# Two tail loads in 256-byte pieces, and all engine orders planned anew

## The chip, the cores and the metric

One NeuronCore of a Trainium2 chip runs the whole program. The metric is device time in microseconds (us), the median of the runs shown; before the change it is 316.97 us. TensorE (PE) does the matmuls and transposes, VectorE (DVE), ScalarE (ACT) and GpSimd (POOL) do the element-wise work, and SyncE (SP) issues the loads and stores, which sixteen DMA engines carry out.

## The reference

Sliding-window attention feeds a two-layer block. There are 8 batches, 8 heads, 576 tokens and 64 numbers per head; inputs and output are float32.

```python
scores = q @ k.T / sqrt(64)                # per batch and head, 576 x 576
scores = where(abs(i - j) <= 32, scores, -1e9)
attn = softmax(scores)                     # over the last axis
x = (attn @ v)                             # heads side by side: 4608 x 512
h = maximum(x @ w_in, 0)                   # w_in 512 x 2048
out = (s * h * h + b) @ w_out              # w_out 2048 x 512, s and b are scalars
```

## The kernel before

All matmuls work on bf16 with float32 sums in PSUM, which the program divides into four tiles of two banks each: `w`, `o`, `sc` and `avn`. The program is not written in the order in which it runs. Each step is recorded as a task with `add` (stream, functions, an assumed cost, what it reads and writes, a key, and for loads a number of packets and a cost of each), and `_Graph.plan` then walks through time: it always takes the open task that could start first, with the key as tie-break, and so fixes one order for each of five streams (PE, ACT, DVE, POOL, SP). Some constants at the head of the file are such keys; others say which engine does a cast or a copy and which bank is used. `fill` looks for gaps that are planned on PE and puts dummy matmuls into them (`ONESW` times `ONESW`, of 128 columns at L563 or 512 at L564). `emit` turns dependencies into semaphore waits. At run time each engine keeps its order, and only the waits decide when something starts. A second path of the program runs only on inputs that the first one's sums flag as out of range.

The first 70 us differ from the rest, because nothing is loaded yet. Loads of batches 0 and 1 and of both weights go through SP in one firm order (keys under -100; the lists `ORDER0` and `ORDER1`). For each batch these are:

- four pairs of heads, for q and for k (`load_pair`, L724): 512 tokens, 256 KB, in packets of 1 KB, each into one of eight staging slots (`STG`);
- the last 64 tokens of all heads, q and k (`load_rest`, L737), called the tails here;
- v (L668, for batch 0 also L685).

Between them stand w_in and w_out (`load_weights`, L640) in chunks of 512 KB, two loads each, in packets of 2 KB. A firm load's number is its place in that order, counted from nought in the constants of the change; by the words "third" and "twelfth" the loads with numbers 2 and 11 are meant. Number 11 is the second load of w_in.

What is staged is cast to bf16 (L757 for q, k and tails, L643 for weights, L677 for v) and, for q and k, transposed on PE: `turn_pair` (L770, four 128 x 128 transposes, copied out at L776) and `turn_rest` (L788, copied out at L798 and L799). Scores follow (L1016, for the last tokens L1047), exponentials (L1061), the mask (L1066; for batch 0 the scores' banks are opened with the mask's large negatives instead, L1035), the product of weights and values (L940), the divisors (L964) and the normalising (L966), a transpose to `xt` (L973) and its copy (L981).

The slots are used in turn. The casts of batch 1's pairs are recorded after all firm loads, so where a slot is loaded twice, a pair's cast waits for the slot's second load: pair 2 for loads of w_out, pair 1 for the loads of pair 3, which are the last two pair loads of all.

The block's first product is `s1` (L1213), with relu on ACT (L1220) and the square on DVE (L1222); its second product is `s2` (L1231), put out with s and b at L1247 and stored. For the first 512 tokens the second product is cut into 32 groups of two matmuls, which add up in four banks (`o` and `avn`) and which PE takes up while it waits for loads (`early`, L1264); their results go out at L1276 (ACT) or L1279 (DVE). `colsum` (L1294) sums w_out's columns for the term with b.

From batch 2 on, q and k are transposed by DMA (`piece`); the first `XPE` units of attention have their results transposed on PE, the later ones by DMA.

The loads of the tails before, and the turn of the tails before, are these lines:

```python
stg[:, 256 * x:256 * x + 256],
src[b, :, BODY:S, :].rearrange("h (p i) d -> h p (i d)", i=ROWS)
...
tile[p0:p0 + 64, 64 * j:64 * j + 64].rearrange("p (a s) -> p a s", a=NPAIR), lhsT=nat[:, 64 * j:64 * j + 64],
```

Each load has 8 heads x 16 partitions, four tokens (1 KB) on a partition: 128 packets. The turn makes sixteen matmuls with pieces of the identity, each into 64 partitions.

Of the kernel before, what the change touches and what calls it, by code (L numbers as in the profile page):

```python
# [7 lines left out]
BF16 = mybir.dt.bfloat16  # L8
# [3 lines left out]
S = 576  # L12
D = 64
H = 8
DM = H * D
DFF = 2048
WIN = 32
NPAIR = H // 2
# [4 lines left out]
VW = 66  # L23
QB = 176
LAG = 1
SPLIT = (4, 3)
WHOLE = 9
SPREAD = ('act', 'dve', 'act', 'act')
K0 = ('dve', 'dve', 'pool', 'pool')
Q0 = ('dve', 'dve', 'act', 'dve')  # L30
# [3 lines left out]
PLACEK = (-28.3, -27.4, -24.3)  # L34
PLACEB = ('AVN', 'W', 'W')
BANK0 = ('AVN', 'SC', 'O', 'SC', 'O')
SCORE0 = ('SC', 'O', 'SC', 'O', 'SC')
OPENK = -55
LASTK = -21.3
WINE = ('dve', 'act', 'pool', 'pool')  # L40
TURNKEY = -18.5
TURN = (None, 0)
FIRST = ((0, 0), (None, 0), (1, 1), (0, 1), (1, 0), (0, 2), (1, 2), (2, 0), (2, 1), (2, 2), (0, 3), (2, 3), (None, 0), (None, 0), (None, 0), (1, 3), (None, 0))
WOUTE = (('act', 'pool'), ('act', 'pool'), ('act', 'dve'), ('pool', 'dve'))
TAIL = ('dve', 'act')
HOST = (("k", 3), ("q", 0))
HELD = (3400.0, 1200, 2800, 4000)
OPEN = -19.25
REST = ('dve', 'dve')
ORDER1 = (('w', 0), ('w', 1), ('p', 2), ('p', 1), ('p', 0), ('w', 3), ('w', 2), ('e', 0), ('p', 3), ('v', 2), ('v', 4), ('v', 3), ('v', 0), ('v', 1))  # L50
XTS = 2500
EARLYW = (('W', 0), ('W', 1), ('W', 0), ('AVN', 1), ('W', 1), ('AVN', 1), ('SC', 0), ('O', 0), ('O', 0), ('W', 1), ('AVN', 1), ('W', 1), ('AVN', 1), ('W', 1), ('SC', 0), ('W', 1), ('O', 1), ('W', 1), ('AVN', 0), ('AVN', 0))
SUMS = -20
PREP = -17.5
SUME = 'act'
SUMC = 'dve'
EARLYP = ('act', 'dve', 'dve', 'act')
ADDE = ('pool', 'dve', 'dve', 'dve')
ADDK = 11.0
SUMAT = 3  # L60
ROWS = 4
BODY = 128 * ROWS
XPE = 20
LEAD = 10.0
SIZES = (224, 128, 160, 256, 256)
PACE = ((-1, -1, -1),) * 3
CASTS = 40.0
LATE = 8
CASTE = (("pool", "pool"), ("pool", "pool"))
SLACK = (2500.0, 1000.0, 4500, 1000)  # L70
PACEV = ((-1,-1,0,0,1),(0,0,1,1,2),(0,0,1,1,2))
EV0 = ('act', 'pool', 'act', 'act', 'act')
BANK1 = ('SC', 'W', 'O', 'SC', 'AVN')
EV1 = ('pool', 'dve', 'pool', 'pool', 'dve')
EV2 = ('pool', 'pool', 'pool', 'dve', 'dve')

ACT_TABLE_SET_ID = 6
FAR = 1e38
COPYQ = (('act', 'dve', 'act', 'dve'), ('act', 'act', 'dve', 'act'))
COPYK = (('dve', 'act', 'act', 'act'), ('dve', 'act', 'act', 'act'))  # L80
XTE = ('dve', 'act', 'act', 'dve', 'act', 'act', 'act', 'act', 'dve', 'dve', 'act', 'act', 'dve', 'act', 'act', 'act', 'act', 'act', 'dve', 'act')
TURN1 = (1, 0, 3, 1, 2, 3, 0, 2, 1)
SCORE1 = ('SC', 'SC', 'SC', 'W')
FIRSTQK = (('qk', 'kq', 'kq', 'qk'), ('qk', 'qk', 'qk', 'kq'))
K1 = ('pool', 'dve', 'dve', 'dve')
Q1 = ('pool', 'pool', 'pool', 'dve')
SUMBANK = ("W", 1)
WARM = 5
LEAST = 2.0 ** -60
AHEAD = {"pe": 48, "act": 180, "dve": 240, "pool": 240}  # L90

# [17 lines left out]
class _Graph:  # L109
# [55 lines left out]
    def plan(self):  # L165
# [5 lines left out]
        for t in self.tasks:  # L171
            for d in t.deps:
                d.users.append(t)
        open_ = {s: [t for t in self.tasks if t.left == 0 and t.stream == s] for s in self.STREAMS}
        order = []
        shape, pair = "full", {"dve": 0.0, "pool": 0.0}
# [53 lines left out]
        while len(order) < len(self.tasks):  # L230
            best = None
            for s in self.STREAMS:
                for t in open_[s]:
# [14 lines left out]
            t = best[1]  # L248
# [29 lines left out]
        while any(rings.values()):  # L278
            done, clock[0] = serve(rings, clock[0], 1e9)
            done.fin = clock[0] + self.WRITE  # L280
        self.fill()

    def fill(self):

        pe = [t for t in self.order if t.stream == "pe"]
        at = {t: i for i, t in enumerate(self.order)}
        new = []
        for i in range(1, len(pe)):
            a, b = pe[i - 1], pe[i]
# [24 lines left out]
        for i, t in reversed(new):  # L314
            self.order.insert(i, t)
# [93 lines left out]
def bass_sliding_window_symmetric__then__act_starrelu_kernel(  # L409
# [23 lines left out]
    with ExitStack() as es:  # L433
# [24 lines left out]
        STG = [STGS[:, i, :] for i in range(NSTG)]  # L458
# [21 lines left out]
        IDENT = sb((128, 128), BF16, "ident")  # L480
# [104 lines left out]
        for p0 in (0, 64):  # L585
# [1 line left out]
        ones = ONESW.rearrange("p (one c) -> p one c", one=1).to_broadcast((128, 4, 128))  # L587
        add("pe", [lambda e, bank=bank: e.matmul(bank.rearrange("p (a c) -> p a c", a=4), lhsT=ONESW[:, :], rhs=ones,
                                                 start=True, stop=True)
                   for bank in (SC[:, 0, :], SC[:, 1, :], O[:, 0, :], O[:, 1, :], W[:, 1, :])],  # L590
            430.0 * WARM, reads=["ONESW"], writes=[("W", 1), ("SC", 0), ("SC", 1), ("O", 0), ("O", 1)], key=-99)

        def mask_of(c, u):
# [126 lines left out]
        def load_pair(b, name, pr, load_key):  # L720

            si = take("stg", NSTG)
            land["pair", b, name, pr] = si
            add("sp", lambda e: e.dma_start(  # L724
                STG[si][:, 0:512].rearrange("p (h c) -> p h c", h=2),
                src_of[name][b, 2 * pr:2 * pr + 2, 0:BODY, :].rearrange("h (p i) d -> p h (i d)", i=ROWS)),
                600.0, writes=[("STG", si)], key=load_key, dma=("l", 16, 95.0 if (b, name, pr) == (0, "q", 1) else 47.0))
# [53 lines left out]
        def turn_rest(b, key, banks, waits=()):  # L781
# [6 lines left out]
            add("pe", [lambda e, j=j, p0=p0: e.matmul(  # L788
                tile[p0:p0 + 64, 64 * j:64 * j + 64].rearrange("p (a s) -> p a s", a=NPAIR), lhsT=nat[:, 64 * j:64 * j + 64],
                rhs=heads[:, p0 // 64, :, :], start=True, stop=True, skip_group_check=True)  # L790
                for j in range(2 * ROWS) for p0 in (0, 64)],
                480.0, reads=[("NAT", ni), "IDENT"], writes=[res], key=key, waits=waits)
# [815 lines left out]
```

## Time and profile before

| what | value |
|---|---|
| runs | 316.97, 315.79, 319.0 us (median 316.97) |
| the profiled execution | 319.02 us, its span 317.3 us |
| granted TensorE clock, mean over the span | 0.989 |
| PE busy | 300.5 us (95%) |
| DVE, ACT, POOL busy | 184.4, 147.5, 109.5 us |
| loads and stores | 98469 packets, 56.08 MB |

The span is the profiled stretch of the program; the execution's own time is a little longer than its span. "Busy" is the time in which an engine runs instructions. The table of slices divides the span into 40 equal parts and gives for each the share of busy time in tenths. The granted clock says at which part of its full speed TensorE was allowed to run. The chain of work that ended last is followed back from the last instruction, so that its pieces are what the end of the program depended on; an engine that is idle beside the chain costs nothing. All durations come from one execution.

### The profile page before, as it was taken

To read this page: it belongs to the slowest core of one execution; us is meant where nothing else is said; L and a number is where in the kernel's file an instruction comes from. 1 tells how busy PE (TensorE), PEld (TensorE's weight loads), DVE (VectorE), ACT (ScalarE), POOL (GpSimd) and SP (SyncE) were. 2 spreads that over 40 slices of the span, in tenths; PEclk is the share of its full clock that TensorE was granted. 3 is DMA by queue.
4 is the path that set the end of the run, shared out by engine and by line. 5 is a ranking of instruction groups with operands and counts; after the bars stand their busy time and mean duration, and the time that the engine had idled before them with its cause. 6 is when DMAs were issued, how large, how long until landed. Compare 5 with 4: busy or idle time off the path is not lost.

```text
span 317.3 us, 7989 instructions
## 1 busy us (share of the span) xinstructions
PE 300.5 (95%) x3356; PEld 162.5 (51%) x3396; DVE 184.4 (58%) x364; ACT 147.5 (46%) x230; POOL 109.5 (35%) x142
## 2 busy tenths in 40 slices
PE   6989979999999999999999999999999999999995
PEld 2558935477664445454545444444444444444444
DVE  5555575469886865768469846776544453323312
ACT  2866757355453665555257317634444433333300
POOL 4208523876374337627523670467000000000000
PEclk9989997999999999999999999999999999999999
DMA  6999999993998899799899979997321211001022
GB/s 211 344 341 382 347 259 275 188 191 94 295 220 165 280 193 181 175 275 180 141 278 167 186 165 298 217 193 174 82 56 53 68 33 61 33 33 36 34 99 69
DMA packets 98469, 56.08 MB, mean 177 GB/s; under 512 B 69952, under 2 KB 89664, under 8 KB 98432
## 3 DMA queue, kind: packets, MB, share of 16 engines
q1 hardware_dynamic: 98432, 55.56, 73.5%
q8 instruction: 27, 0.44, 0.6%
q14 instruction: 10, 0.08, 0.1%
HBM read 36.70 MB, written 9.44 MB: 145 GB/s over the span
## 4 chain that ended last, share of the span: by engine, by line
PE 84%; DMA 9%; issue 2%; DVE 2%; ACT 1%; SPq 1%; POOL 0%
PE w L1213 36%; PE o L1231 34%; DMA stg<-in_k_dram 4%; PE avn L940 4%; DMA stg<-in_moe_w_in_dram 3%; PE o L1264 2%; PE sc L882 2%; DMA stg<-in_q_dram 2%; PE avn L1264 1%; PE avn L973 1%; ACT r L1220 1%; DVE xn L966 1%; PE avn L1213 1%; PE o L940 1%; PE sc L940 0%
## 5 line engine op out<-in xcount | busy, mean ns | idle before, releaser
L1213 PE MATMUL w<-xt,win 128*128 128x512 bf16 (+4 forms) x642 | 131.9, 342 | 2.3 <-ACT r L1220 1.3
L1220 ACT ACTIVATE r<-w 128x512 bf16<-128x512 f32 (+2 forms) x137 | 80.8, 591 | 101.4 <-PE w L1213 93.4
L1222 DVE TENSOR_TENSOR gt<-r 128x512 bf16<-128x512 bf16 (+2 forms) x148 | 78.4, 541 | 79.6 <-ACT r L1220 79.2
L1231 PE MATMUL o<-wout,gt 128*128 128x512 bf16 (+1 forms) x507 | 121.0, 372 | 2.4 <-issue 2.1
L1213 PEld LDWEIGHTS w<-xt,win 128*128 128x128 bf16 x656 | 60.6, 98 | 53.4 <-ACT r L1220 1.3
L1231 PEld LDWEIGHTS o<-wout,gt 128*128 128x128 bf16 x528 | 50.2, 98 | 53.5
L831 POOL CAST nat<-stg 128x1024 bf16<-128x1024 f32 (+1 forms) x36 | 40.8, 1132 | 50.6 <-DMA stg<-in_q_dram 33.7
L910 ACT ACTIVATE ex<-sc 128x1024 bf16<-128x1024 f32 (+1 forms) x28 | 28.7, 1024 | 22.2 <-PE avn L940 21.0
L848 POOL COPY kt<-ktr 128x512 bf16<-128x512 bf16 (+1 forms) x30 | 31.2, 1041 | 17.9 <-DMA ktr<-nat 16.5
L1247 DVE SCALAR_TENSOR_TENSOR outs<-o,sb,cvec 128x512 f32<-128x512 f32 (+1 forms) x33 | 24.0, 729 | 18.7 <-PE o L1231 18.6
L914 DVE TENSOR_TENSOR ex<-ex,mask 128x1024 bf16<-128x1024 bf16 (+1 forms) x28 | 22.0, 786 | 1.9 <-ACT ex L910 1.1
L966 DVE TENSOR_TENSOR xn<-avn,rec 128x512 bf16<-128x512 f32 (+1 forms) x30 | 20.6, 688 | 0.8
L940 PE MATMUL avn<-vb,ex 64*64 64x65 bf16 x912 | 19.2, 197 | 0.1
L940 PEld LDWEIGHTS avn<-vb,ex 64*64 64x64 bf16 x912 | 12.5, 106 | 13.0 <-issue 10.2
L677 POOL CAST vb<-vst 128x512 bf16<-128x512 f32 x21 | 15.0, 714 | 9.9 <-DMA vst<-in_v_dram 9.1
L882 PE MATMUL sc<-qt,kt 64*64 64x128 bf16 x432 | 11.4, 216 | 0.0
L1264 PE MATMUL avn<-wout,gt 128*128 128x512 bf16 x30 | 9.1, 416 | 0.1
L757 POOL CAST nat<-stg 128x512 bf16<-128x512 f32 x6 | 4.2, 699 | 12.9 <-DMA stg<-in_k_dram 8.6
L964 DVE RECIPROCAL rec<-avn 128x8 f32<-128x8 f32 (+1 forms) x30 | 6.0, 200 | 4.5 <-PE avn L940 4.3
L757 DVE CAST nat<-stg 128x512 bf16<-128x512 f32 x11 | 5.2, 476 | 4.5 <-DMA stg<-in_k_dram 3.1
L1264 PE MATMUL o<-wout,gt 128*128 128x512 bf16 x29 | 7.3, 380 | 0.5 <-issue 0.5
L882 PEld LDWEIGHTS sc<-qt,kt 64*64 64x64 bf16 x432 | 7.5, 107 | 0.0
(163 smaller groups left out, 188.7 us busy)
## 6 DMA issues: line engine op xcount, KB each, us to landing
out_dram<-outs SPq DMA_DIRECT2D x35, 256.0 KB, 2.5
vst<-in_v_dram SPq DMA_DIRECT2D x28, 256.0 KB, 5.4
stg<-in_k_dram SPq DMA_DIRECT2D x6, 1024.0 KB, 10.7
stg<-in_q_dram SPq DMA_DIRECT2D x6, 1024.0 KB, 5.7
stg<-in_moe_w_in_dram SPq DMA_DIRECT2D x8, 512.0 KB, 9.7
stg<-in_moe_w_out_dram SPq DMA_DIRECT2D x8, 512.0 KB, 7.8
stg<-in_q_dram SPq DMA_DIRECT2D x8, 256.0 KB, 5.7
stg<-in_k_dram SPq DMA_DIRECT2D x8, 256.0 KB, 5.5
```

The costliest lines, as they stand in the source:

```text
L831: add(eng, lambda e, x=x: e.tensor_copy(nat[0:top, 1024 * x:1024 * x + 1024].rearrange("p (i h d) -> p h i d", h=H, i=2), stg[0:top, :].re ...
L848: add("pool", lambda e, c=c, w=w: e.tensor_copy(KT[slot][:, :, c:c + w].rearrange("p a (s i) -> p a s i", i=4), KTR[slot][:, :, :, c // 4: ...
L882: fns = [lambda e, pr=pr, x=x, b=b, j=j, hp=hp: e.matmul(SC[64 * x:64 * x + 64, hp, pr * 128:pr * 128 + 128], lhsT=KT[b % 2][64 * hp:64 * ...
L910: add("act", lambda e, dst=flat_dst, src=flat_src: e.activation(dst, src, AF.Exp, bias=0.0, scale=0.125), 170 + 0.833 * 512 * len(hs), rea ...
L940: return [lambda e: e.matmul(av[64 * x:64 * x + 64, h, 0:D + 1], lhsT=buf[64 * g:64 * g + 64, h % 2, h // 2, c:c + 64], rhs=VB[64 * g:64 * ...
L966: add("dve", lambda e: e.tensor_tensor(XN[xi][0:p1, :].rearrange("p (a c) -> p a c", a=H), av[0:p1, :, 0:D], REC[ri][0:p1, :].rearrange("p ...
L1213: add("pe", [lambda e, g=g, kc=kc: e.matmul(wt[:, g, :], lhsT=WIN_BF[:, kc, (f0 + g) * 128:(f0 + g + 1) * 128], rhs=XT[:, kc, t0 % XR:t0 % ...
L1220: add("act", lambda e: e.activation(rt, wt, AF.Relu, bias=0.0, scale=1.0), 170 + 0.833 * ng * nt, reads=[(name, wb)], writes=[("R1", rb)], ...
L1222: add("dve", lambda e: e.tensor_tensor(GT[gs][:, f0:f0 + ng, g0:g0 + nt], rt, rt, ALU.mult), 155 + 0.53 * ng * nt, form="two", reads=[("R1 ...
L1231: add("pe", [lambda e, fc=fc: e.matmul(O[:, ob, 0:cn], lhsT=GT[gs][:, fc, g0:g0 + 128], rhs=WOUT_BF[:, fc, c0:c0 + cn], start=(fc == 0), s ...
L1247: add("dve", lambda e: e.scalar_tensor_tensor(OUTS[us][:, 0:cn], bank, SB128[:, 0:1], CVEC[:, c0:c0 + cn], ALU.mult, ALU.add), 210 + 1.05 ...
L1264: add("pe", [lambda e, fc=fc, bank=bank, gs=gs, g0=g0: e.matmul(bank, lhsT=GT[gs][:, fc, g0:g0 + 128], rhs=WOUT_BF[:, fc, :], start=(fc == ...
```

## The change

Three things change.

*The tails.* Each load brings 8 heads x 64 tokens in pieces of one token and one head, 256 bytes, into every second partition, q on the even ones and k on the odd ones: 512 packets for each load. The cast is as before in size. A tail is then turned with four whole 128 x 128 transposes into bf16, and the copies pick the even columns for q and the odd ones for k.

*The planner.* While planning, the cost of the firm loads' packets is multiplied by `SLOW`, and the loads of `EXTRA` are assumed to take 1000 and 500 ns more; afterwards the old values are put back. `fill` fills `FILLED` of a gap. The warm-up has six matmuls instead of five (`WARM`).

*The constants.* Nearly all keys and choices of engine and bank are new, and so the orders of all streams. On SP the sequence of loads is the same but for q and k within pairs (the third load is now q, and the last pair of batch 1 is loaded q first) and for w_out's chunk 2 ahead of chunk 3. The loads of batch 1's pair 0 now go into slots that DVE casts w_out's first chunk from (before: ACT and POOL). The tail of batch 0 and its v rest are cast on POOL, as is w_in's second chunk. On PE, 24 matmuls of `early` stand ahead of the transposes of batch 1's pair that waits for the last pair loads (18 before), and the dummies behind the warm-up are 8 of 512 columns (12 before).

```diff
-SPLIT = (4, 3)
+SPLIT = (3, 2)
...
-WINE = ('dve', 'act', 'pool', 'pool')
+WINE = ('dve', 'pool', 'pool', 'pool')
...
-WOUTE = (('act', 'pool'), ('act', 'pool'), ('act', 'dve'), ('pool', 'dve'))
+WOUTE = (('dve', 'dve'), ('pool', 'act'), ('act', 'dve'), ('pool', 'dve'))
...
-REST = ('dve', 'dve')
+REST = ('pool', 'dve')
...
-EARLYP = ('act', 'dve', 'dve', 'act')
+EARLYP = ('dve', 'act', 'act', 'dve')
...
+SLOW = 1.0
+EXTRA = ((2, 1000.0), (11, 500.0))
+FILLED = 0.6
...
-XPE = 20
-LEAD = 10.0
+XPE = 18
+LEAD = 9.0
...
-FIRSTQK = (('qk', 'kq', 'kq', 'qk'), ('qk', 'qk', 'qk', 'kq'))
-K1 = ('pool', 'dve', 'dve', 'dve')
-Q1 = ('pool', 'pool', 'pool', 'dve')
+FIRSTQK = (('qk', 'qk', 'kq', 'qk'), ('qk', 'qk', 'kq', 'qk'))
+K1 = ('act', 'pool', 'dve', 'dve')
+Q1 = ('pool', 'dve', 'dve', 'dve')
...
-WARM = 5
+WARM = 6
...
+        firm = {t: t.dma for t in self.tasks if t.dma is not None and t.key < -100}
+        for i, t in enumerate(sorted(firm, key=lambda t: t.key)):
+            t.dma = t.dma[0], t.dma[1], SLOW * t.dma[2] + dict(EXTRA).get(i, 0.0) / t.dma[1]
...
+        for t in firm:
+            t.dma = firm[t]
...
-            count = int((b.start - st - self.GUARD) / each)
+            count = int(FILLED * (b.start - st - self.GUARD) / each)
...
-                stg[:, 256 * x:256 * x + 256],
-                src[b, :, BODY:S, :].rearrange("h (p i) d -> h p (i d)", i=ROWS)) for x, src in enumerate((q, k))],
-                1200.0, writes=[("STR", b)], key=load_key, dma=("l", 16, 50.0), waits=[land["paired", b]] if b else [])
+                stg[x:128:2, :].rearrange("s (h d) -> s h d", h=H), src[b, :, BODY:S, :].rearrange("h s d -> s h d"))
+                for x, src in enumerate((q, k))], 1200.0, writes=[("STR", b)], key=load_key, dma=("l", 64, 20.0),
+                waits=[land["paired", b]] if b else [])
...
-            view = tile.rearrange("p (x i a s) -> p x a s i", x=2, i=ROWS, a=NPAIR)
-            heads = IDENT.rearrange("p (a two s) -> p two a s", a=NPAIR, two=2)
-            add("pe", [lambda e, j=j, p0=p0: e.matmul(
-                tile[p0:p0 + 64, 64 * j:64 * j + 64].rearrange("p (a s) -> p a s", a=NPAIR), lhsT=nat[:, 64 * j:64 * j + 64],
-                rhs=heads[:, p0 // 64, :, :], start=True, stop=True, skip_group_check=True)
-                for j in range(2 * ROWS) for p0 in (0, 64)],
-                480.0, reads=[("NAT", ni), "IDENT"], writes=[res], key=key, waits=waits)
+            view = tile.bitcast(BF16)[:, 0:512].rearrange("p (a c) -> p a c", a=NPAIR)
+            add("pe", [lambda e, pr=pr: e.transpose(view[:, pr, :], nat[:, pr * 128:pr * 128 + 128], IDENT[:, :])
+                       for pr in range(NPAIR)], 225.0, reads=[("NAT", ni), "IDENT"], writes=[res], key=key, waits=waits)
...
-            for name, dst, src in (("QT", QT[slot][:, :, WIN + BODY:WIN + S], view[:, 0, :, :, :]),
-                                   ("KT", KT[slot][:, :, BODY:S], view[:, 1, :, :, :])):
-                dst = dst.rearrange("p a (s i) -> p a s i", i=ROWS)
+            both = view.rearrange("p a (s x) -> p a x s", x=2)
+            for name, dst, src in (("QT", QT[slot][:, :, WIN + BODY:WIN + S], both[:, :, 0, :]),
+                                   ("KT", KT[slot][:, :, BODY:S], both[:, :, 1, :])):
```

In the line numbers of the profile after, a step stands 4 to 8 lines lower (L770 is L778, L788 is L795, L1264 is L1268).

More of the change, by code (lines that the diff above doesn't have):

```diff
@@ L25 @@
 LAG = 1
-SPLIT = (4, 3)
+SPLIT = (3, 2)
 WHOLE = 9
-SPREAD = ('act', 'dve', 'act', 'act')
-K0 = ('dve', 'dve', 'pool', 'pool')
-Q0 = ('dve', 'dve', 'act', 'dve')
+SPREAD = ("act", "act", "dve", "dve")
+K0 = ('dve', 'dve', 'pool', 'dve')
+Q0 = ('dve', 'dve', 'dve', 'act')
 ORDER0 = (('p', 0), ('p', 1), ('p', 2), ('p', 3), ('r', 0), ('r', 1), ('w', 0), ('v', 4), ('e', 0), ('w', 1), ('w', 2), ('w', 3))
@@ L33 @@
 ROWE = ("pool", "dve")
-PLACEK = (-28.3, -27.4, -24.3)
+PLACEK = (-27.8, -28.2, -21.9)
 PLACEB = ('AVN', 'W', 'W')
 BANK0 = ('AVN', 'SC', 'O', 'SC', 'O')
-SCORE0 = ('SC', 'O', 'SC', 'O', 'SC')
-OPENK = -55
-LASTK = -21.3
-WINE = ('dve', 'act', 'pool', 'pool')
-TURNKEY = -18.5
+SCORE0 = ('SC', 'SC', 'SC', 'O', 'SC')
+OPENK = -30
+LASTK = -23.8
+WINE = ('dve', 'pool', 'pool', 'pool')
+TURNKEY = -17.5
 TURN = (None, 0)
-FIRST = ((0, 0), (None, 0), (1, 1), (0, 1), (1, 0), (0, 2), (1, 2), (2, 0), (2, 1), (2, 2), (0, 3), (2, 3), (None, 0), (None, 0), (None, 0), (1, 3), (None, 0))
-WOUTE = (('act', 'pool'), ('act', 'pool'), ('act', 'dve'), ('pool', 'dve'))
-TAIL = ('dve', 'act')
+FIRST = ((0, 0), (None, 0), (1, 1), (0, 1), (1, 0), (1, 2), (0, 2), (2, 0), (2, 1), (2, 2), (0, 3), (2, 3), (None, 0), (1, 3), (None, 0), (None, 0), (None, 0))
+WOUTE = (('dve', 'dve'), ('pool', 'act'), ('act', 'dve'), ('pool', 'dve'))
+TAIL = ('act', 'act')
 HOST = (("k", 3), ("q", 0))
-HELD = (3400.0, 1200, 2800, 4000)
-OPEN = -19.25
-REST = ('dve', 'dve')
-ORDER1 = (('w', 0), ('w', 1), ('p', 2), ('p', 1), ('p', 0), ('w', 3), ('w', 2), ('e', 0), ('p', 3), ('v', 2), ('v', 4), ('v', 3), ('v', 0), ('v', 1))
+HELD = (4000, 800, 2400, 4000)
+OPEN = -18.25
+REST = ('pool', 'dve')
+ORDER1 = (('w', 0), ('w', 1), ('p', 2), ('p', 1), ('p', 0), ('w', 2), ('w', 3), ('e', 0), ('p', 3), ('v', 2), ('v', 4), ('v', 3), ('v', 0), ('v', 1))
 XTS = 2500
[L52 to L56, printed above, removed]
-EARLYP = ('act', 'dve', 'dve', 'act')
+EARLYW = (('W', 1), ('W', 1), ('AVN', 0), ('AVN', 1), ('W', 1), ('AVN', 1), ('SC', 0), ('O', 1), ('O', 0), ('SC', 1), ('AVN', 1), ('SC', 0), ('AVN', 1), ('W', 1), ('O', 0), ('W', 1), ('O', 1), ('W', 1), ('AVN', 0), ('AVN', 0))
+SUMS = -16.0
+PREP = -20.5
+SUME = 'pool'
+SUMC = 'act'
+EARLYP = ('dve', 'act', 'act', 'dve')
 ADDE = ('pool', 'dve', 'dve', 'dve')
-ADDK = 11.0
+ADDK = 8.0
 SUMAT = 3
+SLOW = 1.0
+EXTRA = ((2, 1000.0), (11, 500.0))
+FILLED = 0.6
 ROWS = 4
 BODY = 128 * ROWS
-XPE = 20
-LEAD = 10.0
+XPE = 18
+LEAD = 9.0
 SIZES = (224, 128, 160, 256, 256)
@@ L69 @@
 CASTE = (("pool", "pool"), ("pool", "pool"))
-SLACK = (2500.0, 1000.0, 4500, 1000)
+SLACK = (2500.0, 1500.0, 5000, 1000)
 PACEV = ((-1,-1,0,0,1),(0,0,1,1,2),(0,0,1,1,2))
-EV0 = ('act', 'pool', 'act', 'act', 'act')
+EV0 = ('act', 'pool', 'act', 'act', 'pool')
 BANK1 = ('SC', 'W', 'O', 'SC', 'AVN')
-EV1 = ('pool', 'dve', 'pool', 'pool', 'dve')
-EV2 = ('pool', 'pool', 'pool', 'dve', 'dve')
+EV1 = ('pool', 'pool', 'dve', 'dve', 'dve')
+EV2 = ('dve', 'pool', 'pool', 'pool', 'dve')
 ACT_TABLE_SET_ID = 6
 FAR = 1e38
-COPYQ = (('act', 'dve', 'act', 'dve'), ('act', 'act', 'dve', 'act'))
-COPYK = (('dve', 'act', 'act', 'act'), ('dve', 'act', 'act', 'act'))
-XTE = ('dve', 'act', 'act', 'dve', 'act', 'act', 'act', 'act', 'dve', 'dve', 'act', 'act', 'dve', 'act', 'act', 'act', 'act', 'act', 'dve', 'act')
+COPYQ = (('act', 'act', 'act', 'dve'), ('act', 'dve', 'act', 'act'))
+COPYK = (('dve', 'act', 'act', 'dve'), ('dve', 'act', 'act', 'dve'))
+XTE = ('dve', 'act', 'act', 'dve', 'act', 'act', 'act', 'act', 'dve', 'dve', 'act', 'dve', 'act', 'act', 'act', 'act', 'act', 'act', 'act', 'act')
 TURN1 = (1, 0, 3, 1, 2, 3, 0, 2, 1)
 SCORE1 = ('SC', 'SC', 'SC', 'W')
-FIRSTQK = (('qk', 'kq', 'kq', 'qk'), ('qk', 'qk', 'qk', 'kq'))
-K1 = ('pool', 'dve', 'dve', 'dve')
-Q1 = ('pool', 'pool', 'pool', 'dve')
+FIRSTQK = (('qk', 'qk', 'kq', 'qk'), ('qk', 'qk', 'kq', 'qk'))
+K1 = ('act', 'pool', 'dve', 'dve')
+Q1 = ('pool', 'dve', 'dve', 'dve')
 SUMBANK = ("W", 1)
-WARM = 5
+WARM = 6
 LEAST = 2.0 ** -60
@@ L589, in bass_sliding_window_symmetric__then__act_starrelu_kernel @@
                                                  start=True, stop=True)
-                   for bank in (SC[:, 0, :], SC[:, 1, :], O[:, 0, :], O[:, 1, :], W[:, 1, :])],
+                   for bank in (SC[:, 0, :], SC[:, 1, :], O[:, 0, :], O[:, 1, :], W[:, 1, :], W[:, 1, :])],
             430.0 * WARM, reads=["ONESW"], writes=[("W", 1), ("SC", 0), ("SC", 1), ("O", 0), ("O", 1)], key=-99)
@@ L726, in load_pair @@
                 src_of[name][b, 2 * pr:2 * pr + 2, 0:BODY, :].rearrange("h (p i) d -> p h (i d)", i=ROWS)),
[L727 removed]
+                600.0, writes=[("STG", si)], key=load_key, dma=("l", 16, 47.0))
             if (name, pr) == HOST[b]:
```

## The prediction

> **What bounds the kernel now.** I read the page first, from its span, its engines and its slices.
>
> ```profile
> span 317.3 us, 7989 instructions
> PE 300.5 (95%) x3356; PEld 162.5 (51%) x3396; DVE 184.4 (58%) x364; ACT 147.5 (46%) x230; POOL 109.5 (35%) x142
> PE   6989979999999999999999999999999999999995
> PEclk9989997999999999999999999999999999999999
> PE 84%; DMA 9%; issue 2%; DVE 2%; ACT 1%; SPq 1%; POOL 0%
> ```
>
> TensorE is busy for 95% of the span and makes 84% of the chain that ended last; loads make 9%. Each slice is 7.93 us (317.3 / 40). The seventh shows busy 7 and clock 7, and the third and fourth show clock 8 and 9. So what can be won lies in the first 70 us. I therefore cut the span at those places, in a table of stretches. Its columns are the length, the busy time of PE, PE's weight loads, DVE, ACT and POOL, then the granted clock, the DMA share and GB/s.
>
> ```profile
> 4.25:7.66 3.41, 2.11 (x21) 1.24 (x19) 1.50 (x4) 0.62 (x2) 0.71 (x3) 1.00 0.92 274
> 17.90:21.31 3.41, 2.29 (x62) 1.56 (x61) 2.67 (x9) 2.52 (x5) 0.00 (x0) 1.00 1.04 362
> 21.31:24.73 3.42, 3.42 (x32) 2.14 (x31) 1.19 (x3) 2.23 (x4) 0.61 (x4) 0.50 1.05 386
> 24.73:45.21 20.48, 19.70 (x290) 16.73 (x290) 13.58 (x32) 14.56 (x27) 11.86 (x24) 1.00 1.05 345
> 45.21:48.62 3.41, 1.02 (x11) 0.66 (x11) 1.86 (x5) 0.90 (x2) 0.88 (x2) 1.00 0.77 145
> 48.62:52.03 3.41, 3.41 (x26) 1.93 (x27) 1.50 (x3) 2.34 (x5) 2.25 (x3) 0.50 1.05 258
> 66.06:280.00 213.94, 208.73 (x2344) 108.37 (x2367) 137.63 (x256) 101.06 (x154) 79.41 (x78) 1.00 0.76 162
> ```
>
> Two stretches of 3.41 us ran at clock 0.50, so each lost up to 3.41 / 2 = 1.7 us of work. Each stands right behind a stretch in which PE was little busy: 2.29 of 3.41 us, and 1.02 of 3.41. From 66 to 280 us PE is busy 208.73 of 213.94 us, which leaves 5.2 us at most. The stretch with 1.02 us is the largest hole. Its cause stands in the chain of waits (start, length, what) and in PE's timeline (the bracket is the idle time before, and who ended it):
>
> ```profile
> 38.50 8.31 DMA stg<-in_k_dram
> 46.81 0.05 issue
> 46.86 0.88 POOL nat L757
> 47.74 0.05 issue
> 47.79 0.40 PE o L770 x4
> ...
> 45.02 0.38 PE L1264 MATMUL avn<-wout,gt 128*128 128x512 bf16 x1
> 47.79 0.40 PE L770 MATMUL o<-ident,nat 128*128 128x128 bf16 x4 [2.39 <-POOL nat L757]
> ```
>
> The k load issued at 38.50 lands at 46.81, POOL casts it in 0.88, and PE stands idle for 2.39 us until 47.79. This is the first load of the last q/k pair of batch 1. It fills a staging slot that an earlier pair's cast shares, so the transposes of that pair wait for it.
>
> **The change, part by part.** All sums are against the profiled execution: span 317.3, reported time 319.02, so 1.72 us lie outside the span. That execution is 2.05 us above the median of 316.97, the upper end of the three runs.
>
> *The stall at 45 us.* Three things work on it. First, what PE does ahead of it: in the order of before, 18 early second products (L1264) stand ahead of the waiting transposes; in that of after, 24. Second, the cast that PE waits for is on DVE instead of POOL. Third, the loads.
>
> ```profile
> 62.62 0.86 PE o L1264 x4
> 19.56 0.43 DVE L757 CAST nat<-stg 128x512 bf16<-128x512 f32 x1
> ```
>
> Six matmuls at 0.86 / 4 = 0.215 us are 1.29 us; DVE's cast is 0.88 - 0.43 = 0.45 shorter. That leaves 2.39 - 1.29 - 0.45 = 0.65 us of the stall for the loads to close. For them I read the DMA view over three windows (packets, volume, rate):
>
> ```profile
> DMA packets 858, 0.70 MB, mean 233 GB/s; under 512 B 455, under 2 KB 683, under 8 KB 858
> DMA packets 1814, 3.48 MB, mean 386 GB/s; under 512 B 123, under 2 KB 123, under 8 KB 1813
> DMA packets 1804, 0.50 MB, mean 249 GB/s; under 512 B 1766, under 2 KB 1803, under 8 KB 1803
> ```
>
> These are 14.5:17.5 us, where the tails of batch 0 travel in 1 KB packets with a v load of 256 B packets; 20:29, where nearly all packets are 2 KB; and 49:51, where nearly all are 256 B. The first took 3.0 us for what the second rate would carry in 0.70 / 0.386 = 1.8, so 1.2 us are the price of the slow packets in that window. The new tails are 2 x 64 x 8 x 256 B = 0.26 MB. At the third rate they take 1.05 us; the other 0.44 MB at the full rate take 1.14; together 2.19 against 3.0, a gain of 0.8 us. The queue stays full until the 45 us stall (DMA share 1.05 from 24.73 to 45.21), so a load that is earlier at 17 us is earlier at 46 too. The second pair of tails lies among v loads of 256 B that are slow anyway, so I take a third of that, 0.3. Bounds for both: nothing (256-byte pieces take as long) and 2.0 (the 1.2 at the first, 0.8 at the second). I take 1.1, the rate row's answer. That is over 0.65, so the stall goes: **-2.4 us**. The next load behind it was issued 0.5 us later:
>
> ```profile
> 38.50 0.45 SPq L724 DMA_DIRECT2D stg<-in_k_dram  x1
> 39.00 0.47 SPq L724 DMA_DIRECT2D stg<-in_q_dram  x1
> stg<-in_q_dram SPq DMA_DIRECT2D x1, 256.0 KB, 8.7
> ```
>
> It lands at 39.00 + 8.7 = 47.7, then 46.6; with POOL's 0.88 that is 47.5. PE comes to it after two groups of transposes and one of L1264, at 45.40 (where the 2.39 began) + 1.29 + 2 x 0.22 + 0.43 = 47.6: just in time, so what is late next is this load, with 0.1 to spare.
>
> The Trainium skill, "DMA: Bandwidth & Descriptors", section "Specifications", speaks against this part: transfers under 512 B don't reach line rate. The third rate above agrees, 249 against 386 GB/s. By that rule alone the tails would cost 0.26 / 0.249 - 0.26 / 0.386 = 0.37 us more than full-rate packets, an estimate. What it doesn't tell is that the 1 KB tails stood in a window slower still, 233.
>
> *The half clock behind it.* With 2.39 us less idle, the stretch 45.21:48.62 would be busy as its neighbours are, and 48.62:52.03 has no reason to be halved: **-1.7**. Bounds: 0 and -1.7. The stretch 21.31:24.73 I leave as it is, since its forerunner changes little.
>
> The Trainium skill, "TensorE: Matmul & The Clock Gate", section "What's actually happening", puts half rate behind at least one idle window of 3.4 us. The trace has the length, but halves after 2.29 busy us of 3.41, and after 2.11 (4.25:7.66) the next is full. By that rule a stall of 2.39 us would cost no clock; the measured rows decide here.
>
> *The tail turn.* Sixteen matmuls become four, in each of two batches:
>
> ```profile
> 55.05 0.37 PE w L788 x16
> 48.18 0.22 PE w L770 x4
> ```
>
> 0.37 - 0.22 = 0.15 each: **-0.3**. The copies behind it read the same 256 columns per partition from bf16 instead of f32, 0.37 us on ACT either way, and the matmuls of L1264 that follow cover them.
>
> *The front.* DVE's divisors stand behind the cast of the twelfth load, in both programs:
>
> ```profile
> 17.37 0.69 DVE L643 CAST win<-stg 128x1024 bf16<-128x1024 f32 x1 [1.62 <-DMA stg<-in_moe_w_in_dram]
> 17.98 0.20 DVE L964 RECIPROCAL rec<-avn 128x8 f32<-128x8 f32 x1
> 18.96 0.40 PE L973 MATMUL avn<-ident,xn 128*128 128x128 bf16 x4 [0.90 <-DVE xn L966]
> ```
>
> PE idles 0.90 us for it. The twelfth load is ahead of the tails on the queue but shares the engines with them. Bounds 0 and -0.9; I take half, **-0.4**. The tail cast and one w_in cast go to POOL, which is idle here (0.00 busy from 17.90 to 21.31).
>
> *Fewer fillers left at 62 us.* What was done earlier can't hide a wait later. The banks of the first second products are emptied by a put (ACT or DVE) before the next product of weights and values may write there:
>
> ```profile
> 62.66 0.59 ACT L981 COPY xt<-w 128x512 bf16<-128x512 bf16 x1 [0.18 <-PE w L973]
> 63.14 0.69 ACT L1276 ACTIVATE outs<-o,sb 128x512 f32<-128x512 f32 x1
> ```
>
> In before, eight matmuls of L1264 and eight of L1213 (64.35, 0.87 us) run between those transposes and the next product; in after, the order has none. One such put, 0.69, is exposed: **+0.7**; bounds 0 and 0.59 + 0.69 = 1.3.
>
> *Two transposes more by DMA.* The count of unit transposes issued by SP goes from 19 to 21, so PE has 2 x 0.22 less in a stretch where it is 98% busy: **-0.4**; bounds +0.5, if one comes late, and -0.4. The casts that change engine, the reordered first blocks and the banks cost nothing: from 24.73 to 45.21 DVE, ACT and POOL are busy 13.58, 14.56 and 11.86 of 20.48 us. If that cover went, one 1.0 us cast on the path would be the price.
>
> **Sum**: -2.4 - 1.7 - 0.3 - 0.4 + 0.7 - 0.4 = -4.5. The span becomes 312.8, the time 319.02 - 4.5 = **314.5 us**, 2.5 us (0.8%) under the median.
>
> **The rivals.** *The pieces are no faster.* The change then doesn't do what it says. PE comes to the wait at 46.7 and goes on at 46.81 + 0.05 + 0.43 + 0.05 = 47.3; the second load costs 47.7 + 0.88 - 48.2 = 0.4 more; with 1 us idle in that stretch the half clock can stay: 314.5 + 0.65 + 0.4 + 1.7 = 317.2. For it: 249 and 233 GB/s lie close together. Against: the other 0.44 MB in the window.
>
> *Everything comes early.* The loads gain the full 2.0, the first halved stretch goes as well, and the put is hidden: PE comes to the wait 1.7 earlier, but the load holds it at 46.81 - 2.0 + 0.5 = 45.3, 1.0 before the forecast's 46.3. So 314.5 - 1.0 - 0.7 = 312.8.
>
> *Fewer dummy matmuls, a colder clock: slower.* The dummies (L563, L564) fill 60% of each gap instead of all; 12 of 512 columns behind the warm-up become 8.
>
> ```profile
> L564 PE MATMUL avn<-onesw 128*128 128x512 bf16 x5 | 1.6, 381 | 0.0
> ```
>
> Four fewer at 1.6 / 5 = 0.32 are 1.3 us less of busy clock before 21 us. If stretches at 2.3 busy us are the point from which the next is halved, three more of the five before 21.31 can fall under it, at 1.7 each, and what PE loses there comes behind the loads: with the stretch at 48.62 halved too, 314.5 + 4 x 1.7 = 321.3. It decides from the third stretch on. For it: 2.29 was not enough. Against: 2.11 was, and the dummies are few in all.
>
> **How the numbers follow.** Forecast 0.42, pieces no faster 0.26, everything early 0.15, colder clock 0.17. About 1% is what a measurement of this kernel can tell, as the runs before spread from 315.79 to 319.0. Faster by over 1% is below 313.8: all of the early case and 0.08 of the forecast's, 0.23. Slower, above 320.1: 0.16. The rest, 0.61. The range reaches from the early case, 312.8, to 319.0, over the case of slow pieces with one more stretch halved (317.2 + 1.7 = 318.9); it leaves out the colder clock.
>
> **What the profile after would show.** The idle time before the waiting transposes of the last pair (now L778) under 0.7 us; the stretch behind them at clock 1.00; the k and q loads landing 1.1 us earlier; the tail turn at 0.22; a wait of PE on such a put near 62 us. The forecast is wrong if the granted clock shows 0.50 more than once, or if PE waits for another load, for instance because the loads of batch 1's pair 0 now wait for DVE's casts of w_out.

## The result, and the profile after

The changed kernel takes 314.69 us in the median of 20 runs (313.04 to 317.48); the kernel before, run beside it 20 times, takes 318.29 us (315.79 to 320.37). The ratio is 0.9887, with a 95% interval of 0.9862 to 0.9911: 1.1% faster. The forecast was 314.5 us. The median of before had moved from 316.97 (three runs) to 318.29 (twenty), so the gain is 3.6 us rather than the 2.5 that stood in the prediction. The profiled execution of after took 316.08 us, 1.4 over its median. Runs over 1.5% above the fastest of the same kernel are left out of the ratios and intervals, and a ratio can differ by up to 0.3% from the quotient of the two medians.

The page of after, the same lines as before:

```profile
span 314.3 us, 7925 instructions
PE 296.1 (94%) x3320; PEld 159.9 (51%) x3361; DVE 192.2 (61%) x366; ACT 144.1 (46%) x229; POOL 110.4 (35%) x142
PE   6899999989999999998999989999999999999995
PEclk9999999999999999999999999999999999999999
PE 78%; DMA 9%; DVE 7%; issue 2%; ACT 1%; SPq 1%; POOL 0%
```

The hole in the seventh slice is gone, and so are the two slices at clock 7 and 8. DVE, 2% of the chain before, is 7% of it now. The stretches of before, cut at the same times (length, busy time of PE, PE's loads, DVE, ACT and POOL, granted clock, DMA share, GB/s):

```profile
17.90:21.31 3.41, 3.23 (x60) 2.08 (x59) 2.18 (x5) 2.51 (x6) 1.70 (x3) 1.00 1.05 382
21.31:24.73 3.42, 3.35 (x83) 2.54 (x83) 1.50 (x2) 2.81 (x5) 2.86 (x7) 1.00 1.06 386
45.21:48.62 3.41, 2.72 (x27) 1.54 (x26) 2.73 (x7) 1.21 (x3) 0.87 (x1) 1.00 0.90 178
48.62:52.03 3.41, 3.25 (x53) 1.63 (x53) 2.24 (x6) 3.30 (x6) 0.61 (x1) 1.00 0.86 239
66.06:280.00 213.94, 206.67 (x2245) 105.76 (x2277) 138.85 (x247) 100.09 (x152) 80.00 (x79) 1.00 0.81 165
```

PE is busy 3.23 us where it was 2.29, and 2.72 where it was 1.02, and both stretches behind these run at full clock, the one at 21 us too, which the forecast had left halved. Later, from 66 us on, PE is busy 2 us less than before in the same length. The chain of waits round the stall (start, length, what), PE's timeline there, and the issue and flight of the two loads:

```profile
39.37 6.92 DMA stg<-in_k_dram
46.29 0.05 issue
46.35 0.88 POOL nat L765
47.22 0.05 issue
47.27 0.40 PE w L778 x4
...
52.25 0.22 PE w L795 x4
...
45.54 0.40 PE L778 MATMUL o<-ident,nat 128*128 128x128 bf16 x4
47.27 0.40 PE L778 MATMUL w<-ident,nat 128*128 128x128 bf16 x4 [0.56 <-POOL nat L765]
59.91 0.32 PE L944 MATMUL o<-vb,ex 64*64 64x65 bf16 x16 [0.34 <-ACT xt L985]
...
38.32 1.00 SPq L732 DMA_DIRECT2D stg<-in_q_dram  x1
stg<-in_q_dram SPq DMA_DIRECT2D x1, 256.0 KB, 6.7
```

The last pair's loads land at 38.32 + 6.7 = 45.0 and at 39.37 + 6.92 = 46.29; before, at 46.81 and 47.7. The stall of 2.39 us is one of 0.56 now, behind the second load and its cast on POOL. The tail turn takes 0.22, as forecast. The wait on the banks near 60 us is there, with 0.34.

Two waits of PE in this trace are of the size by which this execution lies over the median (who waited, for whom; us in total, times, longest):

```profile
PE avn L944 <- DVE ex L918: 1.1, 1, 1.1
PE o L1235 <- DVE gt L1226: 1.0, 1, 1.0
```

The trace without dummies below has the same orders behind 66 us and neither of the two. That they are the reason isn't shown: another trace with these orders, of 314.88 us, has the second of them too.

### The profile page after: what moved, and what is told of

It reads as the page before. It is cut to its first block, busy times and chain, and to the rows that moved or that the text cites. A ratio compares the mean times of both kernels' runs of the same rounds, so it can differ in the third digit from the quotient of the medians.

```text
span 314.3 us, 7925 instructions
## 1 busy us (share of the span) xinstructions
PE 296.1 (94%) x3320; PEld 159.9 (51%) x3361; DVE 192.2 (61%) x366; ACT 144.1 (46%) x229; POOL 110.4 (35%) x142
## 4 chain that ended last, share of the span: by engine, by line
PE 78%; DMA 9%; DVE 7%; issue 2%; ACT 1%; SPq 1%; POOL 0%
PE o L1235 34%; PE w L1217 33%; DMA stg<-in_q_dram 4%; PE avn L944 4%; DVE gt L1226 3%; DMA stg<-in_moe_w_in_dram 3%; DMA stg<-in_k_dram 2%; PE o L1268 2%; PE sc L886 2%; DVE xn L970 1%; DVE ex L918 1%; ACT r L1224 1%; PE avn L977 1%; SPq L732 1%; PE o L944 0%
## 5 line engine op out<-in xcount | busy, mean ns | idle before, releaser
L1226 DVE TENSOR_TENSOR gt<-r 128x512 bf16<-128x512 bf16 (+2 forms) x148 | 83.6, 577 | 75.1 <-ACT r L1224 74.7
L1217 PE MATMUL w<-xt,win 128*128 128x512 bf16 (+3 forms) x604 | 126.3, 347 | 3.4 <-ACT r L1224 2.1
L1224 ACT ACTIVATE r<-w 128x512 bf16<-128x512 f32 (+2 forms) x134 | 79.5, 593 | 95.0 <-PE w L1217 85.6
L1217 PEld LDWEIGHTS w<-xt,win 128*128 128x128 bf16 x624 | 57.7, 98 | 52.5 <-ACT r L1224 1.9
L835 POOL CAST nat<-stg 128x1024 bf16<-128x1024 f32 (+1 forms) x36 | 40.0, 1111 | 44.9 <-DMA stg<-in_q_dram 27.6
L852 POOL COPY kt<-ktr 128x512 bf16<-128x512 bf16 (+1 forms) x30 | 32.0, 1068 | 20.8 <-DMA ktr<-nat 19.3
L918 DVE TENSOR_TENSOR ex<-ex,mask 128x1024 bf16<-128x1024 bf16 (+1 forms) x28 | 22.9, 816 | 1.2 <-ACT ex L914 0.6
L685 POOL CAST vb<-vst 128x512 bf16<-128x512 f32 (+1 forms) x21 | 15.0, 713 | 20.9 <-DMA vst<-in_v_dram 20.4
L1065 ACT ACTIVATE ex<-sc 128x1024 bf16<-128x1024 f32 (+2 forms) x8 | 7.2, 918 | 3.7 <-PE sc L1020 3.3
L1268 PE MATMUL avn<-wout,gt 128*128 128x512 bf16 x30 | 8.1, 379 | 0.4 <-ACT r L1224 0.2
L685 DVE CAST vb<-vst 128x512 bf16<-128x512 f32 (+1 forms) x13 | 8.0, 618 | 0.0
L1268 PE MATMUL o<-wout,gt 128*128 128x512 bf16 x29 | 7.1, 380 | 0.5 <-issue 0.5
```

What stands on the lines that cost most here:

```text
L685: (lambda e: e.tensor_copy(VB[0:n, vb, :, 0:D], VST[0:n, vs, :, :])),
L835: add(eng, lambda e, x=x: e.tensor_copy(nat[0:top, 1024 * x:1024 * x + 1024].rearrange("p (i h d) -> p h i d", h=H, i=2), stg[0:top, :].re ...
L852: add("pool", lambda e, c=c, w=w: e.tensor_copy(KT[slot][:, :, c:c + w].rearrange("p a (s i) -> p a s i", i=4), KTR[slot][:, :, :, c // 4: ...
L918: add("dve", lambda e, flat=flat, mask=mask: e.tensor_tensor(flat, flat, mask, ALU.mult), 155 + 0.53 * 512 * len(hs), form="two", reads=[( ...
L1217: add("pe", [lambda e, g=g, kc=kc: e.matmul(wt[:, g, :], lhsT=WIN_BF[:, kc, (f0 + g) * 128:(f0 + g + 1) * 128], rhs=XT[:, kc, t0 % XR:t0 % ...
L1224: add("act", lambda e: e.activation(rt, wt, AF.Relu, bias=0.0, scale=1.0), 170 + 0.833 * ng * nt, reads=[(name, wb)], writes=[("R1", rb)], ...
```

## The experiments

All medians below stand beside before on the same chip and hour, which took 318.72, 318.66, 318.23 and 318.41 us in the four groups. A single median of six to twelve runs that spread over 3 us is good to about half a microsecond. After's 314.69 us come from a group of their own, so a difference to it, from one group to another, is good to less than that.

### The tails alone

The kernel before with the new loads and the new turn, planned with the old costs so that all orders stay.

```diff
-stg[:, 256 * x:256 * x + 256], src[...].rearrange("h (p i) d -> h p (i d)", i=ROWS)
+stg[x:128:2, :].rearrange("s (h d) -> s h d", h=H), src[b, :, BODY:S, :].rearrange("h s d -> s h d")
 dma=("l", 16, 50.0)
```

> The kernel before with the new tails (loads and turn) alone; every engine keeps the order of before, since the planner is given the old costs. Theory A (the tails let the loads behind them land 1.1 us earlier, the new orders give the rest): the stall of 2.39 us before the last pair's transposes becomes about 1.3, the tail turns give 0.3, and the halved stretch behind the stall may go: 1.4 to 3.1 us under before, so some 315 to 317 us where before has 318.3. Theory B (the orders do it all, the 256-byte pieces are no faster): the stall stays at 2.4, only the turns' 0.3 us are gained, 318.0 us.

Measured: 315.88 us, ratio 0.9915 (0.9883 to 0.9948), 2.8 us under before. PE's timeline, and the two loads:

```profile
45.95 0.44 PE L770 MATMUL o<-ident,nat 128*128 128x128 bf16 x4 [1.38 <-POOL nat L757]
...
38.61 0.90 SPq L724 DMA_DIRECT2D stg<-in_k_dram  x1
39.55 0.47 SPq L724 DMA_DIRECT2D stg<-in_q_dram  x1
stg<-in_k_dram SPq DMA_DIRECT2D x1, 256.0 KB, 6.4
stg<-in_q_dram SPq DMA_DIRECT2D x1, 256.0 KB, 6.2
```

They land at 45.0 and 45.75, 1.8 and 1.95 us earlier than before, and the stall falls to 1.38. In this trace one stretch behind it, from 46.18 us, is still halved; in four of the six runs the mean clock leaves room for none. Theory A holds; the loads gain more than the 1.1 us that it gave them.

### The new orders alone

The changed kernel with the old loads and turn, planned with the new costs.

```diff
-stg[x:128:2, :].rearrange("s (h d) -> s h d", h=H), src[b, :, BODY:S, :].rearrange("h s d -> s h d")
+stg[:, 256 * x:256 * x + 256], src[...].rearrange("h (p i) d -> h p (i d)", i=ROWS)
 dma=("l", 64, 20.0)
```

> The changed kernel with the old tails (loads and turn); every engine keeps the order of after, since the planner is given the new costs. Theory A: the loads land 1.1 us later, the wait of 0.56 us before the last pair's transposes grows to about 1.7, the turns cost 0.3 more: 1.4 us over after (316.1 where after has 314.7), or 3.1 over if a stretch behind that wait is halved again. Theory B (orders alone): 0.3 us over after, 315.0. If it is within 0.5 us of before (318.3), the orders alone were worth nothing.

Measured: 316.86 us, ratio 0.9946 (0.9919 to 0.9973), 1.9 us under before and 2.2 over after.

```profile
47.98 0.40 PE L778 MATMUL o<-ident,nat 128*128 128x128 bf16 x4 [1.71 <-DVE nat L765]
49.56 0.61 PE L778 MATMUL w<-ident,nat 128*128 128x128 bf16 x4 [0.42 <-POOL nat L765]
```

With the old tails the stall is back, 1.71 + 0.42 us, and a halved stretch behind it, from 49.27 us. The k load of the last pair lands at 48.58, 2.3 us later than in after, where theory A had 1.1. Theory A again: both halves of the change are worth something alone. The two ratios multiply to 0.9861, just outside the interval of the whole (0.9862 to 0.9911), so the halves may overlap a little; the intervals are too wide to tell.

### One KB, but sixteen engines

The outermost dimension of a tail's DRAM pattern is 8 before (the heads) and 64 after (the tokens). Here it is 16, with the pieces still 1 KB.

```diff
-src[b, :, BODY:S, :].rearrange("h (p i) d -> h p (i d)", i=ROWS)
+src[b, :, BODY:S, :].rearrange("h (p i) d -> p h (i d)", i=ROWS)
...
-heads = IDENT.rearrange("p (a two s) -> p two a s", a=NPAIR, two=2)
+heads = IDENT.rearrange("p (s a two) -> p two a s", a=NPAIR, two=2)
```

> The kernel before with the tails still in pieces of 1 KB, but the DRAM pattern's outermost dimension is 16 (the partition) instead of 8 (the head), and the pieces lie on other partitions; sixteen matmuls turn them as before. All orders are the same. If the old tails were slow because 8 of the 16 DMA engines carried them, the loads behind them land 1.1 us or more earlier, as with the new tails, and the stall before the last pair's transposes falls from 2.39 to 1.3 or less: 1 to 3 us under before. If the size of the pieces or the turn matters, nothing changes: within 0.5 us of before.

Measured: 318.35 us, ratio 0.9969 (0.9940 to 0.9998): 0.4 us under before by the medians, 1.0 by the ratio. The loads come early, but the time hardly moves:

```profile
37.63 0.86 SPq L724 DMA_DIRECT2D stg<-in_k_dram  x1
38.53 0.47 SPq L724 DMA_DIRECT2D stg<-in_q_dram  x1
stg<-in_k_dram SPq DMA_DIRECT2D x1, 256.0 KB, 7.9
stg<-in_q_dram SPq DMA_DIRECT2D x1, 256.0 KB, 8.1
...
20.06 1.12 PE L788 MATMUL w<-ident,nat 128*64 128x64 bf16 x16
65.70 0.21 PE L940 MATMUL sc<-vb,ex 64*64 64x65 bf16 x1 [1.73 <-issue]
```

They land at 45.5 and 46.6, 1.3 and 1.1 us before those of before, with the same piece size. In a second trace of this kernel, further below, they land at 45.9 and 46.7, 0.9 and 1.0 earlier, and the stall is 1.23 us. So half or more of what the new tails gain at the loads comes with the 16. Two things take from it here: the turn takes 1.12 us instead of 0.44, and in this execution PE waits 1.73 us near 64 us for nothing that the profile shows.

The records of the single packets agree with half the engines. Batch 0's tails are 256 packets of 1 KB. Before, they travel from 14.55 to 18.77 us and at most 12 of them are under way at one time; here, from 14.20 to 16.43, and at most 22. In the two other traces with 1 KB tails and 8 as the outermost dimension it is at most 11, and in the three others with 16 it is 18 to 19. (Records overlap a little, so these counts lie over the number of engines: packets of 2 KB before, in the same microseconds, come to 20.)

The Trainium skill, "DMA: Bandwidth & Descriptors", section "Why a DMA increments its semaphore by 16 and not by 1", says that a DMA uses the largest number of engines up to 16 that divides the slowest dimension of both its patterns. By that the old tails ran on 8 engines and these on 16, and the packets under way and the landings, 0.9 to 1.3 us earlier, agree.

The same edit in after, under the new orders, and once more beside after itself, unchanged:

> The changed kernel with the old 1 KB pieces, but carried by all 16 DMA engines (outermost dimension 16), and turned by sixteen matmuls; every engine keeps the order of after. Theory C (what the new tails gain is the number of engines, not the size of the pieces): the last pair's loads land within 0.5 us of those of after (45.0 and 46.3), the turns cost 0.3, so within 0.5 us of after (314.7). Theory D (the small pieces and the whole transposes matter by themselves, as the small gain of the 1 KB pieces over 16 engines with the orders of before lets one think): 1.5 to 2.5 us over after, near the orders alone (316.9). If PE then waits for nothing that the profile shows, inside the products of weights and values, for 0.5 us or more, as it did in that run, its own instructions come late once the loads come early.

> The new orders with 1 KB pieces over 16 engines once more, beside after on the same chip. If the size of the pieces matters beyond the engines (theory D), 1 us or more over after. If the 316.3 of the first time was chance (theory C), within 0.7 us of after.

> The changed kernel itself, beside the next one on the same chip: 314.7 us as in its twenty runs, and in the trace the waits of 0.6 us or less at the last pair's transposes and no halved stretch behind them.

Measured: 316.29 us (ratio 0.9931, 0.9899 to 0.9964) and 315.93 us (0.9929, 0.9892 to 0.9966); after itself beside the second, 313.99 (0.9856, 0.9804 to 0.9908), with a wait of 0.51 us at the last pair's transposes and no halved stretch behind it. So the kernels with these loads stay 1.6 and 1.9 us over after, as theory D had it. But the loads themselves do what theory C said, as the first of the two traces shows:

```profile
38.01 0.58 SPq L732 DMA_DIRECT2D stg<-in_q_dram  x1
38.64 0.62 SPq L732 DMA_DIRECT2D stg<-in_k_dram  x1
stg<-in_q_dram SPq DMA_DIRECT2D x1, 256.0 KB, 7.4
stg<-in_k_dram SPq DMA_DIRECT2D x1, 256.0 KB, 7.9
```

They land at 45.4 and 46.5, and in the second trace at 44.9 and 45.9, within 0.5 us of the 45.0 and 46.3 of after; with the new orders and 8 engines the k load landed at 48.58. And PE waits nowhere for more than 0.5 us with nothing that the profile shows. For a part of the time the trace names another cause, the turn, first of the second of these two kernels, then of the kernel of the next section:

```profile
51.82 1.10 PE L796 MATMUL w<-ident,nat 128*64 128x64 bf16 x16
...
51.75 0.45 PE L795 MATMUL w<-ident,nat 128*64 128x64 bf16 x16
```

Both issue sixteen matmuls of the same shape. In the first the identity's columns are read with a step of 8 numbers, because the 1 KB pieces had to lie on other partitions; in the second with a step of 2. That is 0.65 us in each of two batches. The turn of batch 0, near 20 us, stands ahead of the waits for the last pair's loads, and both traces come to the second turn at the same time, 51.82 and 51.75; so only the second turn's 0.65 is seen in them. My edit carried a cost of its own, and some 1 us of the 1.6 to 1.9 stays without a cause, little more than two medians can tell. Theory D is neither shown nor refuted. The fourth corner, 256-byte pieces on 8 engines, wasn't tried.

### The turn alone

The changed kernel with its new loads, turned by sixteen matmuls into float32.

```diff
-e.transpose(view[:, pr, :], nat[:, pr * 128:pr * 128 + 128], IDENT[:, :])
+e.matmul(tile[64 * (h % 2):..., 256 * x + 64 * (h // 2):...], lhsT=nat[:, 64 * h:64 * h + 64], rhs=heads[:, x, :])
```

> The changed kernel with the new loads of the tails, but turned by sixteen matmuls of 64 columns into float32, as before, and copied out from float32; every engine keeps the order of after. By the forecast's step the turn costs 0.15 us more in each of two batches: 0.3 over after (315.0 where after has 314.7). If the whole transposes explain why the 1 KB pieces over 16 engines stayed 1.6 us over after, it comes out at 316 or more.

Measured: 314.24 us, ratio 0.9877 (0.9835 to 0.9918), no slower than after. The turn is worth less than half a microsecond, whatever its rows say, and doesn't explain the 1.6 us of the kernel with 16 engines.

### Clock and dummies

> The changed kernel without the dummy matmuls in the gaps of the first 26 us (the six of the warm-up stay); all other orders are the same. The colder-clock rival: one to three stretches of 3.41 us before 21 us show clock 0.50, at 1.7 us each, 316.4 to 320 us where after has 314.7. Theory A (the clock is held by what stands there anyway): no more than one halved stretch, absorbed by waits for loads, within 1 us of after.

The edit is `FILLED = 0.0`. Measured: 315.42 us, ratio 0.9904 (0.9865 to 0.9942), within 0.8 us of after. The clock did fall, in three stretches before 25 us, each time behind one in which PE had little to do:

```profile
3.95:7.36 3.41, 1.55 (x26) 0.85 (x24) 1.63 (x4) 1.48 (x2) 1.13 (x4) 1.00 0.92 266
7.36:10.78 3.42, 3.28 (x20) 1.72 (x24) 1.13 (x3) 1.30 (x3) 0.61 (x1) 0.50 1.07 366
10.78:17.60 6.82, 4.10 (x104) 2.53 (x107) 4.04 (x8) 5.06 (x9) 1.04 (x1) 1.00 1.17 306
17.60:24.43 6.83, 6.53 (x92) 4.08 (x93) 2.83 (x8) 2.77 (x6) 3.29 (x4) 0.50 1.05 383
...
48.59 0.39 PE L778 MATMUL w<-ident,nat 128*128 128x128 bf16 x4
```

Three halved stretches should cost 5 us at 1.7 each; the median is 0.7 us over after's, and this execution took 314.59. PE comes to the transposes that follow the last pair's second load at 48.59, 1.3 us later than in the trace of after (47.27), and doesn't wait for that load any more. Neither theory had that: the dummies do hold the clock, but the waits for loads up to 47 us take up most of what it costs.

> The kernel before with ten dummy matmuls of 512 columns (2.15 us) put into the stall of 2.39 us ahead of the last pair's transposes; all else keeps its order. It takes the half clock behind the stall away and leaves the wait. By the forecast's price, 1.7 us under before in the runs in which that stretch was halved, about 1 us in the median. By the runs of before, sorted by their mean clock (318.0 with no halved stretch, 318.8 with one, 319.3 with two), 0.6 us for each stretch: 0.3 to 0.6 us under before in the median.

```diff
+hold = _Task(len(g.tasks), "pe", [n.spare[2]] * 10, ...)   # ahead of the waiting transposes, in before
```

Measured: 318.23 us, ratio 0.9982 (0.9957 to 1.0007), 0.4 us under before, if anything. In its trace the stall is filled and no stretch is halved from 27.4 to 68.4 us, and little is gained. The runs of before agree. In the first group of experiments before ran 23 times: ten runs with a mean clock that leaves room for no halved stretch have a median of 318.0 us, six with one 318.8, seven with two 319.3. By that a stretch is worth 0.65 us, not 1.7.

### The fillers and the cast

> The changed kernel with three groups of two early second products (1.29 us) moved from ahead of the last pair's transposes to behind them, as in the order of before; all else keeps its order. By the forecast's step: PE comes 1.29 us earlier to a load that is no earlier, waits 1.29 us more, and ends 1.3 us later, 316.0 where after has 314.7. Rival: the groups fill a later gap (the puts at 59 us), and 0.5 us or less is lost.

```diff
+places = [g.order.index(t) for t in groups[3:]]   # three groups of L1268 move behind the last pair's transposes
```

Measured: 316.19 us, ratio 0.9947 (0.9905 to 0.9988), 1.5 us over after, where the forecast's step said 1.3. The stall of 1.67 us agrees with it:

```profile
46.42 0.40 PE L778 MATMUL o<-ident,nat 128*128 128x128 bf16 x4 [1.67 <-DVE nat L765]
```

> The changed kernel with one cast moved: the k cast of batch 1's pair 1, which waits for the last pair load, runs on DVE just ahead of pair 3's k cast instead of on POOL; all else keeps its order. The wait of 0.56 us of PE behind that cast falls to about 0.1 (0.43 us of DVE in place of 0.88 of POOL). If that wait sets the end, 0.45 us under after (314.2 where after has 314.7); if something behind it (the puts at 59 us, DVE) takes it up, the same as after.

```diff
+cast.stream = "dve"      # pair 1's k cast, just ahead of pair 3's
```

Measured: 314.13 us, ratio 0.9876 (0.9829 to 0.9922). In its trace PE comes to those transposes at 46.86 and waits for nothing. The lead of 0.56 us over after's median is the expected size, but smaller than what these runs can tell; after itself took 313.99 in another group. So it isn't shown to beat after.

### A wait that no row explains

> The kernel before with 1 KB pieces over 16 engines once more, for a second trace. If PE again waits for nothing that the profile shows, near 64 us and in front of the same instruction (in the products of weights and values, the 873rd weight load), the wait belongs to the place in PE's instruction stream: some 0.7 to 2.5 us, with a packet of the instruction queue that starts after 62.5 us. If PE runs through there, that packet starts earlier and the last pair's loads land as in the first trace (45.5 and 46.6), and the time is some 2 us under it, 317 or less.

Measured in one run: 317.37 us. That is 0.4 us more than expected. The wait near 64 us isn't there; the packet of the instruction queue, which in the first trace started at 63.4 us, starts at 60.7. The wait itself appears in a third trace, that of the held clock, in an execution of 323.37 us, at the same place of PE's stream:

```profile
68.75 0.38 PE L940 MATMUL sc<-vb,ex 64*64 64x65 bf16 x11 [2.35 <-issue]
```

There the packet starts at 66.2. In both traces the wait stands in front of the 859th weight load on record (the expectation counted it as the 873rd). The held-clock kernel has ten dummies more ahead of it, so it is the same place and another product. After isn't free of such waits: the second trace of it, an execution of 318.27 us, has one of 2.29 us at 173.92, elsewhere in the stream. Instructions that arrive late would fit all of it, but no run moved that cause, so it stays open.

## Why the prediction was right

The time, the sign and the main mechanism were right: two loads late by their tails, a stall of PE behind them, and work moved ahead of it. By its own steps:

- **The stall, -2.4.** The wait for the first load, now cast on DVE, is gone; 0.56 us stayed behind the second, cast on POOL, for which the forecast had 0.1 to spare. Its parts held: the fillers ahead of it measured about 1.5 (1.29 forecast), and the loads came 1.8 and 1.4 us earlier (1.1 forecast, bound 2.0). The reason that I gave, a slow rate of packets of 1 KB, was the wrong one: pieces of the same 1 KB on 16 engines bring 0.9 to 1.3 us with the orders of before, and under the new orders the k load then lands 2.0 to 2.7 us earlier than on 8. That the term came out near the forecast was in part luck.
- **The half clock, -1.7.** This is the mis-sized term. The stretch goes, in 18 of 20 runs of after there is none at all, but a stretch is worth 0.65 us over the runs of before, and in the held-clock kernel about 0.4, hardly clear of nothing. Half the length of a stretch is a bound, and I took it as the price. The stretch at 21 us, which I left halved, went too.
- **The sum.** Against executions of before with two halved stretches, as the profiled one was (319.3 in the median), after is 4.6 us faster; the forecast had 4.5. Both stretches together make 1.3 of that, where the forecast had 1.7 for one, and everything else 3.3 (318.0 to 314.7, runs without a halved stretch), where the other terms sum to 2.8. The two errors nearly cancel, so it is in part luck that the total is this close.
- **The tail turn, -0.3.** Its rows are as forecast (0.37 to 0.22), its value isn't seen: the old kind of turn in after costs nothing measurable.
- **The front, -0.4.** DVE's cast of the twelfth load starts at 16.79 instead of 17.37, 0.58 us earlier. Its value can't be told from that of the loads.
- **The puts, +0.7.** 0.34 was exposed.
- **Two transposes by DMA, -0.4.** Not seen. From the fifth put of the second product to the last, the kernels with the new orders change their lead over before by between +0.5 and -1.9 us in eight traces (the one with the wait of 2.29 us left out); the -1.9 is the profiled execution of after, with DVE's waits of 1.1 and 1.0 us.

The rivals: that the new tails bring nothing fell with the tails alone (2.8 us), though what the small pieces add to the 16 engines wasn't settled. The colder clock didn't come; with no dummies at all it came as a clock and hardly as a time. "Everything early" was half right, since both halved stretches went, but the put stayed.

## What to carry to other kernels

Ask how many DMA engines a late load runs on: with pieces of the same size, an outermost dimension of 16 instead of 8 brought the loads queued behind it forward by 0.9 to 1.3 us, and by 2.0 to 2.7 under the new orders. What the size of the pieces adds was left open here. Price a halved clock by runs, not by half its length: ahead of a wait for data it cost little. And when an experiment must move data to isolate a cause, time the moved step itself before reading the total, and ask whether a wait behind it takes that time up.

## What the runs showed of the hardware

Sixteen matmuls of 64 columns took 0.45 us with the moving operand read in steps of 2 numbers (4 bytes) and 1.10 us in steps of 8 (16 bytes), with the same shapes. In a halved stretch they took 1.12 (the row at 20.06 us), so the clock wasn't their limit. Three stretches of half clock before 25 us cost about 1 us in a kernel that then waits for loads (0.7 by the medians, 1.3 at 48 us of one trace). Loads with 8 as their outermost dimension had at most 12 packets of 1 KB under way, with 16 up to 22. And PE can stand 1.7 to 2.4 us at one place of its stream in some executions and not in others, with no engine or load to wait for.
